# A transformer block on one core: tiles 0 and 1 as loads of their own, a new stored order, and ten waits of GpSimd on VectorE

## The chip, the cores and the metric

The kernel runs on one core of a Trainium2 chip. The metric is the time of one execution on the device, in microseconds (us), as the median of several runs. The profile is of one execution; its span is the time from the first to the last instruction on the core. Engines are named as in the profile: PE is TensorE's matmul, PEld its weight load, DVE is VectorE, ACT is ScalarE, POOL is GpSimd, SP is SyncE, which here only issues DMAs (SPq).

## What is computed

The input `x` is one batch of S = 2048 rows of D = 448 values in bf16. The block is an attention layer with 16 heads of 28 values and softmax feature maps, followed by a gated feed-forward layer with F = 1792, each behind a layer norm and with a residual:

```python
q, k, v = heads(ln(x) @ wqkv)
pq, pk = q @ w_phi, k @ w_phi                      # per head, 28 x 28
phi_q = concat(softmax(pq), softmax(-pq))          # 56 features
phi_k = concat(softmax(pk), softmax(-pk))
kv, z = phi_k.T @ v, sum_rows(phi_k)               # over all 2048 rows
o = (phi_q @ kv) / (phi_q @ z + 1e-6)
h = x + merge(o) @ wo
out = h + (sigmoid(ln(h) @ w_gate) * (ln(h) @ w_up)) @ w_down
```

`kv` and `z` sum over all rows, so no row's attention output can be formed before the keys and values of all rows are done. The feed-forward part needs no such sum.

## The kernel before

**Tiles and stages.** The 2048 rows are 16 tiles of 128 rows, taken singly or in pairs (`pr`). The stages are:

- Loads and weights. `x` tiles are loaded by `load_x` (`("x", t0)`), `wk` in two pieces, `w_phi` (`wph`), `wv`, `wq` in four and `wo` in eight (`wom`). `w_phi` is folded into the key and query weights: `kT` (PE transpose, L539), `WkT` (copy), `wM` (matmul, L554), `W2` (copy). For the query weights the transpose is a DMA (`wqT`, L500) on SP's queue, from `wq_raw` to `WqT`.
- First layer norm, tile by tile: `bst` (statistics, L582), `agg` (L584), `ve`, `rstd` (a power on POOL, L587), for later tiles `mm` and `nm` (L590, L592), then `xn` (L601 on ACT, L602 on DVE). The normed tile is transposed into `xnT`: tiles 0 to 3 by PE (`xP`, L612, and a copy `xT`), the others in pairs by a DMA on SP (`xT`, L620).
- Keys and values: `pa` and `pb` (L636) are the two halves of a tile's projection (`va`, `vb` for the values of tiles 0 and 1); a `b` half waits for its `a` half. ACT takes the two exponentials `ekp` and `ekm` (L656, L658); `v1` is a copy. DVE sums them (`ss`, L677) and inverts the sums (`rs`, L681); `phi` (L683) multiplies, on DVE or on POOL. `kv` (L695) adds the tile into one bank of PSUM, tile after tile.
- Queries: `qa` and `q` (L735) for a chunk of four tiles and half of the heads, then `eqp` and `eqm` (L745) on ACT, 1024 columns each.
- When all of `kv` is summed, `kvz` (L750, DVE) masks it. `num` (L771) is a tile's numerator and denominator; `ocp` (L424, a copy out of PSUM) is on ACT or DVE. DVE divides in six steps (`rSm`, `rr`, `b`, `c`, `rd`, `o`, L787 to L799), `od` (L818) pads, and `oT` transposes: for pair 0 on PE (`oP`) with copies, otherwise by a DMA (L820).
- Output projection `woa`, `wo_` (L832) for a pair; for pair 0 the residual is added on PE (`wr`, L840), and `hc` copies the sum. For the others DVE adds it (`h`, L862). Then the second layer norm: `bst2`, `agg2`, `ve2` (L870), `rstd2` (POOL, L872), `hn` (L876) and the transpose `hT` (pair 0: `hP` on PE, L886, and copies; others: DMA, L894).
- Feed-forward in chunks of 2, 4, 4, 4 and 2 tiles: `ga` and `gu` (L933) are the gate and up products of one of 14 slices of F, `sig` (ACT, L942) and `hh` (DVE, L950) gate them, `dn` (L967) multiplies with `w_down`, `fin` (L974) adds the residual and `st` stores a tile. The `wd` loads each wait for a `gu` of the first chunk.

**What sets the order.** Every step is a task with an engine (or a choice of two, `engs`), its dependencies and, on PE, a choice of PSUM banks. `ORDER` is a stored list of numbers, one a task: the number divided by 32 is the task's place in the order of creation, its last two bits choose the engine, and the three bits above choose the banks. `stored` reads the list, `emit` walks through it and appends each task to its engine's queue, in front of it the waits that it needs. A wait is on a semaphore that counts the finished tasks of an engine (or on that of a DMA). Each engine runs its queue strictly in order, so an instruction that waits holds up all that stands behind it. A task that takes a bank also waits for the task that emptied that bank last. On PE, dependencies between its own tasks need no wait, apart from a `b` half on its `a` half. Waits of SP hold up the DMAs behind them in the same way.

The task list of before has 884 tasks. POOL's queue has 47 of them: constants, `Wp`, `ve`, `mm`, `rstd`, `nm`, ten of the sixteen `phi`, and the `rstd2` with two `ve2`. DVE has 304, ACT 169, PE 288 and SP 76.

Of the kernel before, what the change touches and what calls it, by code (L numbers as in the profile page):

```python
# [86 lines left out]
"""  # L87


class _Task:  # L90
    __slots__ = ("name", "eng", "occ", "lat", "fn", "deps", "rank", "kind", "banks", "until", "got",
                 "start", "finish", "idx", "bias", "need", "size", "after", "rows", "pace", "behind", "engs")


class _Graph:


    ENGINES = ("sp", "act", "pe", "dve", "pool")
# [222 lines left out]
def build(nc, A_x, A_wqkv, A_w_phi, A_wo, B_w_gate, B_w_up, B_w_down, out):  # L321
# [7 lines left out]
    for n in SIZES:  # L329
        t0 = CH[-1][0] + CH[-1][1] if CH else 0  # L330
# [10 lines left out]
    with ExitStack() as es:  # L341
# [130 lines left out]
        def load_x(t0, t1, **kw):  # L472
            load(("x", t0), x_sb[:, t0:t1, :], x_t[:, t0:t1, :], size=112.0 * (t1 - t0), **kw)
            for t in range(t0, t1):
                x_ld[t] = ("x", t0)
# [552 lines left out]
```

## Time and profile before

| what | value |
|---|---|
| median of 3 runs | 206.85 us (205.95 to 206.87) |
| the profiled execution | 205.79 us |
| its span | 204.0 us |
| PE busy | 196.3 us (96%) |
| DVE busy | 135.3 us (66%) |
| ACT busy | 94.7 us (46%) |
| POOL busy | 34.5 us (17%) |
| bytes read from HBM, written | 8.98 MB, 1.84 MB |
| granted TensorE clock, mean | 1.00 |

The span has 1.79 us less than the execution's own time; the rest lies before the first and after the last instruction. In the profile, a line of a group gives the operation, what it writes and reads, how many there were, the busy time and the mean duration of one; in a timeline each row begins with the start and the duration, and ends with the idle time of the engine before it and what ended that. PE's matmuls are pipelined, so durations of neighbours overlap, and the time of one is better read from start to start.

### The profile page before, as it was taken

To read this page: it belongs to the slowest core of one execution; us is meant where nothing else is said; L and a number is where in the kernel's file an instruction comes from. 1 tells how busy PE (TensorE), PEld (TensorE's weight loads), DVE (VectorE), ACT (ScalarE), POOL (GpSimd) and SP (SyncE) were. 2 spreads that over 40 slices of the span, in tenths; PEclk is the share of its full clock that TensorE was granted. 3 is DMA by queue.
4 is the path that set the end of the run, shared out by engine and by line. 5 is a ranking of instruction groups with operands and counts; after the bars stand their busy time and mean duration, and the time that the engine had idled before them with its cause. 6 is when DMAs were issued, how large, how long until landed. Compare 5 with 4: busy or idle time off the path is not lost.

```text
span 204.0 us, 5395 instructions
## 1 busy us (share of the span) xinstructions
PE 196.3 (96%) x2276; PEld 109.2 (54%) x2276; DVE 135.3 (66%) x304; ACT 94.7 (46%) x169; POOL 34.5 (17%) x51
## 2 busy tenths in 40 slices
PE   7998998998889999999999999999999999999994
PEld 2544554555436985554445555454444555786553
DVE  2979999996999995789949846722455313541412
ACT  2699997999999462444031441202234400442000
POOL 5626973680000300003000100110000000000000
PEclk9999999999999999999999999999999999999999
DMA  5998797673040394311250020050020000200141
GB/s 153 310 289 133 170 152 128 173 245 125 3 101 5 80 190 118 99 45 31 51 127 5 0 51 3 1 125 3 0 74 3 2 0 3 69 3 0 33 158 59
DMA packets 35109, 16.94 MB, mean 83 GB/s; under 512 B 26828, under 2 KB 34060, under 8 KB 35084
## 3 DMA queue, kind: packets, MB, share of 16 engines
q1 hardware_dynamic: 34812, 16.36, 33.7%
q8 instruction: 18, 0.29, 0.6%
q10 hardware_dynamic: 272, 0.23, 0.3%
q14 instruction: 7, 0.06, 0.1%
HBM read 8.98 MB, written 1.84 MB: 53 GB/s over the span
## 4 chain that ended last, share of the span: by engine, by line
PE 81%; DVE 6%; DMA 5%; ACT 4%; SPq 3%; issue 1%; DVEq 0%
PE bank L933 42%; PE bank L967 21%; PE bank L636 5%; PE bank L832 5%; PE bank L735 4%; DMA WqT<-wq_raw 3%; SPq L460 3%; DMA wq_raw<-in_A_wqkv_dram 2%; PE bank L695 2%; DVE phi L683 1%; PE bank L771 1%; ACT v L424 1%; ACT ek L656 1%; ACT ek L658 1%; SPq L500 1%
## 5 line engine op out<-in xcount | busy, mean ns | idle before, releaser
L933 PE MATMUL bank<-xnT,wg_sb 64*128 64x512 bf16 (+1 forms) x490 | 87.5, 333 | 0.2 <-issue 0.2
L933 PE MATMUL bank<-xnT,wu_sb 64*128 64x512 bf16 (+1 forms) x490 | 87.6, 333 | 0.0
L942 ACT ACTIVATE sg_sb<-bank 128x512 f32<-128x512 f32 (+1 forms) x70 | 34.7, 511 | 81.5 <-PE bank L933 75.7
L950 DVE SCALAR_TENSOR_TENSOR hh<-sg_sb,bank 128x512 bf16<-128x512 f32 (+1 forms) x70 | 39.0, 575 | 30.4 <-ACT sg_sb L942 28.2
L933 PEld LDWEIGHTS bank<-xnT,wg_sb 64*128 64x128 bf16 x490 | 45.0, 94 | 20.9 <-issue 3.0
L933 PEld LDWEIGHTS bank<-xnT,wu_sb 64*128 64x128 bf16 x490 | 44.8, 94 | 14.0
L967 PE MATMUL bank<-wd_sb,hh 128*128 128x448 bf16 (+1 forms) x238 | 43.1, 342 | 0.0
L967 PEld LDWEIGHTS bank<-wd_sb,hh 128*128 128x128 bf16 x238 | 22.9, 98 | 20.1 <-DVE hh L950 0.4
L974 DVE SCALAR_TENSOR_TENSOR x_sb<-bank,x_sb 128x448 bf16<-128x448 f32 (+1 forms) x17 | 9.9, 594 | 24.6 <-PE bank L967 24.5
L636 PE MATMUL bank<-Wk,xnT 64*128 64x448 bf16 x112 | 21.7, 350 | 0.2
L636 PE MATMUL bank<-Wv,xnT 64*128 64x448 bf16 x112 | 21.9, 350 | 0.0
L683 POOL TENSOR_TENSOR phi<-ek,rsum 128x896 bf16<-128x896 bf16 x10 | 17.8, 1784 | 8.0 <-DVE rsum L681 7.4
L677 DVE TENSOR_REDUCE ssum<-ek 128x32 f32<-128x896 bf16 x16 | 16.5, 1064 | 0.4 <-ACT ek L656 0.4
L745 ACT ACTIVATE eq<-bank 128x1024 bf16<-128x1024 f32 x16 | 16.7, 1070 | 0.2
L872 POOL TENSOR_TENSOR rs<-rs,neghalf 128x2 f32<-128x2 f32 x8 | 5.6, 697 | 60.0 <-DVE rs L870 59.8
L735 PE MATMUL bank<-xnT,Wq 64*128 64x512 bf16 x112 | 14.3, 377 | 0.0
L832 PE MATMUL bank<-wo_sb,oT 64*128 64x448 bf16 x112 | 13.0, 350 | 0.7 <-DVE rs L870 0.6
L424 ACT CAST opm<-bank 128x960 bf16<-128x960 f32 x13 | 12.1, 976 | 1.4 <-PE bank L771 1.4
L636 PEld LDWEIGHTS bank<-Wk,xnT 64*128 64x128 bf16 x112 | 9.2, 94 | 6.1 <-PE bank L636 1.5
L636 PEld LDWEIGHTS bank<-Wv,xnT 64*128 64x128 bf16 x112 | 9.2, 94 | 4.8 <-ACT WkT L424 0.3
L862 DVE TENSOR_TENSOR x_sb<-bank,x_sb 128x896 bf16<-128x896 f32 x7 | 7.5, 1085 | 3.4 <-PE bank L832 3.4
L658 ACT ACTIVATE ek<-bank 128x448 bf16<-128x448 f32 x16 | 8.8, 558 | 1.2 <-PE bank L636 1.1
(92 smaller groups left out, 170.5 us busy)
## 6 DMA issues: line engine op xcount, KB each, us to landing
wu_sb<-in_B_w_up_dram SPq DMA_DIRECT2D x4, 448.0 KB, 3.5
wg_sb<-in_B_w_gate_dram SPq DMA_DIRECT2D x4, 448.0 KB, 4.2
out_dram<-x_sb SPq DMA_DIRECT2D x15, 112.0 KB, 1.8
wd_sb<-in_B_w_down_dram SPq DMA_DIRECT2D x7, 224.0 KB, 3.0
x_sb<-in_A_x_dram SPq DMA_DIRECT2D x2, 448.0 KB, 4.5
x_sb<-in_A_x_dram SPq DMA_DIRECT2D x3, 224.0 KB, 4.4
wq_raw<-in_A_wqkv_dram SPq DMA_DIRECT2D x4, 128.0 KB, 3.7
Wv<-in_A_wqkv_dram SPq DMA_DIRECT2D x2, 224.0 KB, 4.6
```

The lines of the kernel that those rows point to most:

```text
L424: return e.copy(dst, src) if hasattr(e, "activation") else e.tensor_copy(dst, src)
L636: r = e.matmul(bank[bk][:, 0:D], lhsT=half(xnT, hi)[:, t, k, :], rhs=half(w, hi)[:, k, :], start=(i == 0), stop=(i == 6), tile_position=(6 ...
L658: task(("ekm", t), "act", act_p(D), lambda e, t=t, s=s: e.activation(ek[:, s, 1, :], bank[got(k_at[t][0])[k_at[t][1]]][:, 0:D], ACT.Exp, s ...
L677: task(("ss", t), "dve", dve(896), lambda e, s=s: e.tensor_reduce(ssum[:, s, :].rearrange("p (a h) -> p a h", h=2), ek[:, s].rearrange("p ...
L683: task(("phi", t), None, 1.68, lambda e, t=t, s=s: e.tensor_tensor(phi[:, t % NPHI, :, :, 0:DH, :].rearrange("p a g d h -> p (a g) d h"), ...
L735: r = e.matmul(bank[bb[j]], lhsT=half(Wq2, hi)[:, k, 2 * g:2 * g + 2].rearrange("p c d h -> p (c d h)"), rhs=half(xnT, hi)[:, 4 * c:4 * c ...
L745: task((key, gp, c), "act", act_p(1024), lambda e, gp=gp, c=c, sg=sg, nm=nm: e.activation(eq[c][:, sg, 2 * gp:2 * gp + 2, :], wide[got(nm) ...
L832: r = e.matmul(bank[bb[j]][:, 0:D], lhsT=half(oT, hi)[:, pr % NO, j, k, :], rhs=half(wo_sb, hi)[:, k, :], start=(i == 0 and not res), stop ...
L933: r = e.matmul(bank[b][:, 0:N], lhsT=half(w, hi)[:, k, fs], rhs=half(hnT, hi)[:, t0:t0 + n, k, :], start=(i == 0), stop=(i == 6), tile_pos ...
L942: task(("sig", f_, c), "act", act_p(N), lambda e, j=j, N=N, nm=nm: e.activation(sg_sb[:, j % NSG, 0:N], bank[got(nm)[0]][:, 0:N], ACT.Tanh ...
L950: task(("hh", f_, c), "dve", dve(N), lambda e, j=j, N=N, nm=nm, f_=f_, c=c: e.scalar_tensor_tensor(hhT[c % 2][:, f_, 0:N], sg_sb[:, j % NS ...
L967: r = e.matmul(bank[b][:, c0:c1], lhsT=hhT[c % 2][:, f_, o:o + P], rhs=wd_sb[:, f_, c0:c1], start=(f_ == 0), stop=(f_ == FT - 1))
```

## The change

Three things are changed.

1. `load_x(0, 2)` becomes `load_x(0, 1)` and `load_x(1, 2)`: tiles 0 and 1 have a DMA each (task `("x", 1)` is new, so all later tasks move by one place). The two places that had taken tile 0's load for both tiles, `wr` and `h`, now name both loads.
2. `ORDER` is replaced by another list. All queues change. The table shows the tasks that change engine.

| engine | no longer there | newly there |
|---|---|---|
| SP | `wk`(1), `x`(6) | `x`(1) |
| ACT | `xT`(0), `W2`(1,3), `xn`(7), `xn`(8), `v1`(12), `ocp`(2), `oT`(0,0), `hT`(0,0) | `wk`(1), `x`(6), `xn`(6), `xn`(14), `v1`(13), `ocp`(0), `ocp`(3), `ocp`(8) |
| POOL | `ve`(12), `nm`(12), `phi`(4), `phi`(10), `phi`(14), `ve2`(4) | `ve`(1), `ve`(2), `ve`(4), `mm`(4), `phi`(5), `phi`(13), `ve2`(7) |

What POOL or ACT lose goes to DVE, and what they gain comes from it (the loads apart). PE keeps its 288 tasks in another order. The parts of the new queues that the prediction speaks of:

```
SP, before: x0 wk1 wk0 x4 wph x6 wv1 wv0 wom0 wq3 wq2 wq1 wq0 x8 x12 wqT1 wqT0 xT4 xT6 ...
SP, after:  x1 x0 wph wk0 x4 wq2 wv1 wq3 wv0 wq1 wq0 x8 wom1 x12 wqT1 wom4 wqT0 xT4 xT6 ...
ACT, before: x2 | ACT, after: x2 wk1 x6
SP later, before: oT1 oT2 wd1 oT3 wd3 wd0 hT1 hT2 wd5 oT4 ...
SP later, after:  oT1 oT2 hT1 wd1 oT3 wd0 hT2 wd3 wd2 wd5 wd4 oT4 ...
PE around WqT, before: pa2 pb2 wM(0,1) wM(0,3) wM(0,2) pa5 pa4 pb5 ...
PE around WqT, after:  pa2 wM(0,0) wM(0,1) wM(0,2) pb2 pa4 wM(0,3) pb4 pa5 ...
PE at kvz, before: kv15 qa(0,3) num0 num1 num2 q(0,3) num3 num4 num5 num6 qa(0,2) qa(1,2) num7 ...
PE at kvz, after:  kv15 qa(0,2) num3 num2 num1 num0 qa(0,3) num5 num7 q(0,2) num6 num4 q(0,3) ...
ACT at kvz, before: ocp1 ocp2 ocp4 ocp5 ocp6 eqp(0,3) ocp7 eqp(1,2) oT(0,0) eqp(0,2) ...
ACT at kvz, after:  ocp3 ocp1 ocp0 ocp5 ocp7 ocp6 ocp4 eqp(0,2) eqp(0,3) eqm(0,2) ...
```

3. `TURNS` lists ten pairs. When the queues are written, the first task of a pair (on POOL) also waits for the second (on DVE).

```diff
+TURNS = [(('rstd', 2), ('xn', 0)), (('rstd', 4), ('xn', 3)), (('phi', 1), ('xn', 9)), (('phi', 2), ('xn',
+         10)), (('rstd', 12), ('phi', 3)), (('phi', 5), ('phi', 4)), (('phi', 7), ('xn', 15)), (('phi', 12),
+         ('phi', 10)), (('rstd2', 2), ('od', 3)), (('rstd2', 6), ('o', 7))]
...
         done = self.stored(ORDER) if ORDER.strip() else self.order()
+        for name, first in TURNS:
+            self.tasks[name].need.append(first)
         queues = {e: [] for e in self.ENGINES}
...
-        load_x(0, 2, bias=BIG, engs=EITHER)
+        load_x(0, 1, bias=BIG, engs=EITHER)
+        load_x(1, 2, bias=BIG, engs=EITHER)
...
-                task(("wr", pr), "pe", 0.38, fr, [x_ld[t0], "ident"], banks=PAIRS,
+                task(("wr", pr), "pe", 0.38, fr, [x_ld[t0], x_ld[t0 + 1], "ident"], banks=PAIRS,
...
-                    [("wo_", pr), x_ld[t0], ("xn", t0), ("xn", t0 + 1)])
+                    [("wo_", pr), x_ld[t0], x_ld[t0 + 1], ("xn", t0), ("xn", t0 + 1)])
```

92 rows, old and new, of the table ORDER are left out of this document.

## The prediction

> **What bounds the kernel now.** I read the page first, then a table of each engine's busy time in five stretches, cut at marks of the chain of waits: the first projection after `WqT` (18.3 us), `kvz` (46.8), the first GLU matmul (65.0), the second GLU chunk (78.0).
>
> ```profile
> span 204.0 us, 5395 instructions
> ...
> PE 196.3 (96%) x2276; PEld 109.2 (54%) x2276; DVE 135.3 (66%) x304; ACT 94.7 (46%) x169; POOL 34.5 (17%) x51
> ```
>
> ```profile
> core 0: us, PE busy (x) PEld busy (x) DVE busy (x) ACT busy (x) POOL busy (x), PEclk, DMA share, GB/s
> 0.00:18.30 18.30, 16.42 (x132) 7.59 (x132) 13.31 (x44) 12.48 (x25) 8.80 (x27) 1.00 0.97 235
> 18.30:46.80 28.50, 27.90 (x487) 15.23 (x488) 27.07 (x51) 26.18 (x49) 19.32 (x14) 1.00 0.75 169
> 46.80:65.00 18.20, 16.03 (x326) 8.64 (x326) 17.34 (x41) 17.51 (x22) 0.69 (x1) 1.00 0.22 57
> 65.00:78.00 13.00, 12.83 (x257) 11.35 (x250) 12.19 (x36) 7.17 (x18) 1.65 (x3) 1.00 0.65 134
> 78.00:204.00 126.00, 123.13 (x1094) 66.41 (x1094) 65.38 (x137) 31.39 (x60) 4.06 (x6) 1.00 0.16 40
> ```
>
> In a row the stretch and its length come first, then busy time by engine. PE (TensorE) is the bound of the whole: 126 us of the 204 are GLU matmuls that no edit touches. The change removes no matmul, so it can win only PE's idle time: 18.30 - 16.42 = 1.88 us in the first stretch, then 0.60, 2.17 and 0.17; the 2.87 of the last are nearly all after the last matmul (201.14). Idle time between 18.3 and 78 is thus 2.94 us, the ceiling of what a better order can win there. From 18 to 65 us DVE and ACT are 95% busy too, so an order has little room. The waits behind the idle time, from PE's timeline (idle time and its releaser in brackets):
>
> ```profile
> 17.55 0.76 PE L554 MATMUL bank<-Wp,WqT 112*128 112x112 bf16 x12 [0.51 <-DMA WqT<-wq_raw]
> ...
> 31.41 0.44 PE L695 MATMUL bank<-v,phi 128*64 128x58 bf16 x16 [0.60 <-DVE phi L683]
> ...
> 50.11 0.40 PE L771 MATMUL bank<-kvz,eq 64*128 64x60 bf16 x16 [0.26 <-ACT opm L424]
> 51.00 0.40 PE L771 MATMUL bank<-kvz,eq 64*128 64x60 bf16 x16 [0.49 <-DVE opm L424]
> ...
> 56.17 0.54 PE L840 MATMUL bank<-x_sb,ident 128*128 128x448 bf16 x2 [0.61 <-DVE oT L424]
> ...
> 60.99 0.74 PE L832 MATMUL bank<-wo_sb,oT 64*128 64x448 bf16 x6 [0.58 <-DVE rs L870]
> ```
>
> **The stall that the turns aim at.** The view of the tile `phi` (minimum, median, maximum in ns):
>
> ```profile
> L683 POOL TENSOR_TENSOR phi<-ek,rsum x10: 1682/1692/2148, 18.5 to 43.4; 128x896 bf16<-128x896 bf16 x10
> L683 DVE TENSOR_TENSOR phi<-ek,rsum x6: 558/586/2105, 28.8 to 45.2; 128x896 bf16<-128x896 bf16 x6
> ```
>
> The two extremes meet: POOL's `phi`(7) runs from 28.72 to 30.87 and DVE's `phi`(3) and `phi`(5) from 28.77 to 31.35. `phi`(3) delays POOL by 2148 - 1682 = 0.47, and then POOL holds `phi`(5) up by 2105 - 558 = 1.55; `kv`(5) waits on PE. In the other overlaps (POOL at 39.66 and 43.43, 1.94 each) it is POOL that loses, by 0.26. So one of many meetings cost DVE anything. [...]
>
> **The terms, on PE's time, against this execution.**
>
> 1. Front, to 18.3 us. `x`(1) alone is 112 KB where 224 KB landed at 4.19, and its statistics lead: up to 0.3 us sooner on DVE. Against that, `wk`(0) (issued 1.93, landed 4.4 later, first transpose of it at 6.41) now has `w_phi` and `x`(6) before it, 249 KB at the page's 300 KB a us: 0.8 later, 7.2. ACT gets both queues' work back: `xT`(0) and `W2`(1,3) go to DVE, two copies of 0.45 from start to start, so `W2` is complete at 6.41 + 0.8 + 5.4 - 0.9 = 11.7, as now (11.81). `WqT`: `wq`(2) and (3) have some 324 KB fewer ahead of them, so the first transpose can issue about 1.0 before 10.45; but `x`(12) is still ahead of it in the rings, and `wom`(4) (0.83) now stands between the two transposes. I take the second to land at 17.2 instead of 17.50 (ends: 16.4, and 17.7). Behind it come three `wM` (0.2 each) and now also `pb`(2) (0.57), which before had run ahead of it: the next projection at 17.2 + 1.2 = 18.4, against 18.29. **+0.1 us** (-0.2 to +0.8, the upper end where `wk`(0)'s 0.8 is not made up).
>
> [...]
>
> 2. 18.3 to 46.8. Idle 0.60 now, all at `kv`(5). Here `phi`(5) goes to POOL with a turn behind `phi`(4), and (4), (10), (14) to DVE, 7 on DVE for 6: DVE gives back 1.55 and takes on 0.56 for a `phi`, 0.3 for `ve`(12) and `nm`(12). The stall goes. What is late next: `pa`(11) comes 0.57 sooner (`pb`(9) stands behind it) and needs the banks that ACT frees with `eqm`(0,0) at 29.10, where PE reaches it now at 29.26; some 0.2 us come back. The six turns here (`phi` 1, 2, 5, 7, 12 and `rstd` 12) hold up POOL's queue: behind `phi`(1) and (2) stand `rstd`(12) and `nm`(12), hence `xn`(12), (13), a transpose on SP and the last projections; but POOL is idle for 9.2 us of the 28.5. **-0.4 us** (-0.6, the whole idle time, to +0.6, the same stall made once more by a turn).
>
> 3. 46.8 to 65. Idle 2.17, every gap behind a copy, or a chain of them, on ACT or DVE. `ocp`(0), (3) and (8) go from DVE (1.15 each) to ACT (0.96, 0.88 apart back to back), `ocp`(2) the other way, and the copies `oT`(0,0) and `hT`(0,0) (0.67, 0.60) from ACT to DVE. ACT: 2 x 0.88 - 0.67 - 0.60 = +0.49; DVE: 0.42 + 0.41 - 2 x 1.15 = -1.47. ACT is the busier now (17.51 of 18.20) and gets fuller: seven `ocp`, 7 x 0.88 = 6.2 us, stand ahead of the last four `eq` pairs. The value is nearer to ACT's row: **+0.3 us** (-1.2, where DVE's relief decides, to +0.5).
>
> 4. 65 to 78. `num`(10) moves behind the first GLU matmul, as work (0.24) neither won nor lost; the 0.17 before the second chunk may go. **-0.1 us** (-0.2 to +1.0, see the second rival).
>
> 5. From 78: the same matmuls, last half tile and store; `rstd2`(6)'s turn behind `o`(7) delays tiles whose chunk starts some 5 us after their transpose lands. **0** (±0.2).
>
> Sum: +0.1 - 0.4 + 0.3 - 0.1 = **-0.1 us**, so 205.7 for the profiled execution's 205.79 (204.0 span and 1.79 around it). The median shown, 206.85, is 1.06 above it: **206.7 us**.
>
> **Rivals.** First, faster: the order's balance counts, DVE's 1.47 us in stretch 3 and the stall in 2. For it: DVE releases two of the last four gaps above. Against: ACT is as full. -0.2 - 0.6 - 1.2 - 0.2 = -2.2 at best, about -1.5 likely: 205.3. Chance 0.26.
>
> Second, slower: `hT`(2) lands after its turn. Before the second chunk SP now issues `hT`(1), `wd`(1), `oT`(3), `wd`(0), `hT`(2): each of the last two transposes has a 224 KB load just ahead. A lone transpose lands 2.7 us after issue (`oT`, page), but the one issued at 72.25 behind two such loads took 4.8. Issued at 73.9 it would land at 78.7 instead of 76.6; PE is there at 78.1. With `oT`(3) late for `woa`(3) as well that is +1.0, on top of term 1 at +0.5 and the rest as forecast: +1.4, 208.2. It decides once such a transpose takes over 4.2 us. For it: that 4.8. Against: one load ahead of each, not two. Chance 0.22.
>
> Third, the turns don't do what they say: DVE is held up elsewhere, since all meetings moved. Price 0.60 again, -0.1 becomes +0.5: inside the forecast's band.
>
> **Chances and range.** The measurement can tell about 0.5%, 1.0 us, from no change. Forecast (with the third rival): 0.52, its own range 205.8 to 207.9. Faster 0.26, slower 0.22. The range takes in most of both rivals and the unknown ends: 205.0 to 208.2.
>
> **What would show it.** Right: no `phi` on DVE above 0.7 us; PE's idle time in stretch 2 under 0.4 and in stretch 3 again 2 to 2.7; first GLU matmul at 64.7 to 65.3. Term 1: first transpose of `wk` near 7.2, `wM`(0) near 17.2. Second rival: a gap of over 0.5 before `woa`(3) or the first matmul of the second chunk, released by a DMA. It is wrong if stretch 3 loses a microsecond of idle time, or if the `WqT` transposes move by more than 0.8.

## The result, and the profile after

The changed kernel takes 209.2 us (median of 18 runs, 206.74 to 212.99), the kernel before 206.78 in the same series (18 runs, 205.95 to 209.13). The ratio is 1.0089 with a 95% interval of 1.0066 to 1.0113: 0.89% of 206.8 is 1.8 us, slower. The ratio leaves out the four runs of the changed kernel that took over 1.5% longer than its fastest (210.87 to 212.99 us); with them the medians lie 2.4 us apart. The forecast, no change at 206.7, was wrong, and the result lies above its range (to 208.2). The profiled execution of the changed kernel took 208.05 us with a span of 206.3, the one before 205.79 and 204.0. That of the kernel before lies 1 us under its median and below all its 18 runs; that of the changed kernel lies near the middle of its nine runs at an undisturbed clock (median 208.0, see e5_filled). So the two traces show where time is lost, but with 2.3 us they show some 0.5 us more of it than the ratio's 1.8.

The page of the changed kernel, and its busy time in the five stretches of the prediction (the columns are those shown there):

```profile
span 206.3 us, 5402 instructions
...
PE 195.5 (95%) x2276; PEld 106.5 (52%) x2276; DVE 135.7 (66%) x305; ACT 93.5 (45%) x167; POOL 31.7 (15%) x52
```

```profile
0.00:18.30 18.30, 13.61 (x112) 6.96 (x112) 13.96 (x42) 10.30 (x20) 8.90 (x29) 1.00 1.01 221
18.30:46.80 28.50, 28.43 (x454) 15.21 (x456) 26.62 (x53) 25.57 (x50) 16.90 (x14) 1.00 0.72 178
46.80:65.00 18.20, 15.81 (x344) 8.62 (x337) 16.45 (x40) 18.17 (x22) 0.70 (x1) 1.00 0.22 56
65.00:78.00 13.00, 12.78 (x268) 10.59 (x264) 11.40 (x34) 8.30 (x17) 1.59 (x3) 1.00 0.44 87
```

PE was busy 13.61 us of the first stretch (16.42 before) and 28.43 of 28.50 in the second (27.90 before): the loss is in the front, and the stall of the second stretch is gone. In the third, ACT is busy 18.17 of 18.20.

Stretches cut at fixed times hold different work in the two kernels. So I cut both traces at the same steps of PE's queue, and where one kernel had still to do a step that the other had done, I add that step's time:

| mark on PE | before | after | later by | still owed | loss so far | of this stretch |
|---|---|---|---|---|---|---|
| first `wM` for the query weights | 17.55 | 18.37 | 0.82 | `pb`(2), 0.57 | 1.39 | **+1.39** |
| `kv`(15) | 46.35 | 47.31 | 0.96 | | 0.96 | **-0.43** |
| first GLU matmul | 65.01 | 66.58 | 1.57 | `num`(10), 0.24 | 1.81 | **+0.85** |
| second GLU chunk | 77.98 | 80.17 | 2.19 | | 2.19 | **+0.38** |
| span | 204.0 | 206.3 | 2.3 | | 2.3 | **+0.1** |

The waits on PE that stand behind this (start, duration, and in brackets the idle time and its releaser):

```profile
18.37 0.76 PE L562 MATMUL bank<-Wp,WqT 112*128 112x112 bf16 x12 [1.52 <-DMA WqT<-wq_raw]
...
50.17 0.40 PE L779 MATMUL bank<-kvz,eq 64*128 64x60 bf16 x16 [0.45 <-ACT opm L431]
...
53.62 0.40 PE L779 MATMUL bank<-kvz,eq 64*128 64x60 bf16 x16 [0.45 <-ACT opm L431]
...
78.50 0.93 PE L840 MATMUL bank<-wo_sb,oT 64*128 64x448 bf16 x8 [0.67 <-DMA oT<-o_pad]
```

The first was 0.51 before. The next two stand behind copies on ACT; they are two of seven waits between `kv`(15) and the first GLU matmul that come to 2.31 us (five and 2.10 before). The last is `woa`(3), held by its transpose, as the second rival had it. A tail hides in the durations: a `num` takes 0.23 from start to start when the next matmul follows at once, and 0.40 when PE then waits, so by these two figures a stop costs about 0.17 that counts as busy, beside the idle time shown.

Why the query weights' transposes came late is read from SP's timeline (start, duration of the issue, what). First the changed kernel, then the kernel before:

```profile
8.34 0.59 SPq L467 DMA_DIRECT2D x_sb<-in_A_x_dram  x1
8.97 0.83 SPq L467 DMA_DIRECT2D wo_sb<-in_A_wo_dram  x1
9.86 0.40 SPq L467 DMA_DIRECT2D x_sb<-in_A_x_dram  x1
10.38 1.33 SPq L508 DMA_TRANSPOSE WqT<-wq_raw  x1
11.76 0.87 SPq L467 DMA_DIRECT2D wo_sb<-in_A_wo_dram  x1
12.73 1.69 SPq L508 DMA_TRANSPOSE WqT<-wq_raw  x1
```

```profile
8.48 1.60 SPq L460 DMA_DIRECT2D x_sb<-in_A_x_dram  x2
10.45 3.54 SPq L500 DMA_TRANSPOSE WqT<-wq_raw  x2
```

`wq`(2) and `wq`(3), which the first transpose needs, had landed at 9.89 (10.44 before), but SP reached it only at 10.38, because it was still issuing. The `wo` load in the middle, `wom`(4), puts the second transpose at 12.73 (11.88 before). It lands at 18.32 (17.50 before).

### The profile page after: what moved, and what is told of

It reads as the page before. It is cut to its first block, busy times and chain, and to the rows that moved or that the text cites. A ratio compares the mean times of both kernels' runs of the same rounds, so it can differ in the third digit from the quotient of the medians.

```text
span 206.3 us, 5402 instructions
## 1 busy us (share of the span) xinstructions
PE 195.5 (95%) x2276; PEld 106.5 (52%) x2276; DVE 135.7 (66%) x305; ACT 93.5 (45%) x167; POOL 31.7 (15%) x52
## 4 chain that ended last, share of the span: by engine, by line
PE 78%; DVE 8%; SPq 5%; DMA 5%; issue 1%; POOL 0%; ACT 0%; POOLq 0%
PE bank L941 37%; PE bank L975 21%; PE bank L644 8%; SPq L467 5%; PE bank L840 4%; PE bank L743 3%; DMA WqT<-wq_raw 3%; DMA oT<-o_pad 2%; PE bank L703 2%; DVE b_sb L802 1%; DVE b_sb L799 1%; DVE o_pad L807 1%; SPq L508 1%; DVE hh L958 1%; DVE opm L431 1%
## 5 line engine op out<-in xcount | busy, mean ns | idle before, releaser
L950 ACT ACTIVATE sg_sb<-bank 128x512 f32<-128x512 f32 (+1 forms) x70 | 34.2, 512 | 79.8 <-PE bank L941 73.5
L941 PEld LDWEIGHTS bank<-xnT,wu_sb 64*128 64x128 bf16 x490 | 45.3, 94 | 16.6
L691 POOL TENSOR_TENSOR phi<-ek,rsum 128x896 bf16<-128x896 bf16 x9 | 15.2, 1690 | 10.1 <-DVE xn_pad L610 3.4
L753 ACT ACTIVATE eq<-bank 128x1024 bf16<-128x1024 f32 x16 | 15.8, 1073 | 0.6 <-PE bank L743 0.6
L431 ACT CAST opm<-bank 128x960 bf16<-128x960 f32 x15 | 13.6, 982 | 4.4 <-PE bank L779 4.4
L590 DVE BATCH_NORM_STATS2 st<-x_sb 128x6 f32<-128x448 bf16 x16 | 9.3, 610 | 2.9 <-DMA x_sb<-in_A_x_dram 2.9
```

The source lines that it names most:

```text
L431: return e.copy(dst, src) if hasattr(e, "activation") else e.tensor_copy(dst, src)
L691: task(("phi", t), None, 1.68, lambda e, t=t, s=s: e.tensor_tensor(phi[:, t % NPHI, :, :, 0:DH, :].rearrange("p a g d h -> p (a g) d h"), ...
L753: task((key, gp, c), "act", act_p(1024), lambda e, gp=gp, c=c, sg=sg, nm=nm: e.activation(eq[c][:, sg, 2 * gp:2 * gp + 2, :], wide[got(nm) ...
L941: r = e.matmul(bank[b][:, 0:N], lhsT=half(w, hi)[:, k, fs], rhs=half(hnT, hi)[:, t0:t0 + n, k, :], start=(i == 0), stop=(i == 6), tile_pos ...
L950: task(("sig", f_, c), "act", act_p(N), lambda e, j=j, N=N, nm=nm: e.activation(sg_sb[:, j % NSG, 0:N], bank[got(nm)[0]][:, 0:N], ACT.Tanh ...
```

## The experiments

All are timed against the kernel before, by ratios with 95% intervals; 0.1% is 0.2 us. My theory: the order's places in the front, in the third stretch and at `oT`(3) cost the time, and the turns nothing. Rivals: the turns hold POOL back; or an idle PE lowers its own clock.

### The turns alone taken out (e1_no_turns)

```diff
-TURNS = [(('rstd', 2), ('xn', 0)), ...
+TURNS = []
```

> The changed kernel with an empty list of turns; the order and the split loads stay. My theory is that the 1.8 us are lost in three places of the order (the query weights' transposes and pb(2) behind them in the front, about 1.2 us; an ACT that is busy 18.17 of 18.20 us between 46.8 and 65, about 0.6; oT(3) late for woa(3), about 0.7) and that the turns cost and win next to nothing: within 0.4 us of the changed kernel, so about 1.0085 of the kernel before. The rival: the turns hold POOL's queue back (rstd, nm and so xn behind them), and the time is theirs: 1.5 us or more comes back, 1.002 or less. The opposite is possible too: without the turns two or three phi on DVE rise above 1.5 us and it becomes slower by 0.5 to 1.5 us.

Measured 1.0109 (1.0061 to 1.0157): the loss stays, so the turns are not its cause. DVE's `phi` in this run (minimum, median, maximum in ns):

```profile
L687 DVE TENSOR_TENSOR phi<-ek,rsum x7: 560/564/624, 26.7 to 46.6; 128x896 bf16<-128x896 bf16 x7
```

None is long. It was 2105 at most in the kernel before, and 626 in the changed one. So the new order removed the stall; with it, the turns had nothing left to do.

### One turn in the kernel before (e13_before_turn)

```diff
+        self.tasks[("phi", 7)].need.append(("phi", 5))
```

> The kernel before with one turn: phi(7) on POOL also waits for phi(5) on DVE, the pair that meets at 28.7 us there (phi(5) takes 2.11 us in place of 0.56, and kv(5) waits 0.60 on PE). If a turn does what it says, no phi on DVE is above 0.7 us, the 0.60 before kv(5) goes, and the kernel is 0.3 to 0.6 us faster (0.997 to 0.9985). The rival: the stall goes, but PE then waits the 0.6 at the next place (ACT and DVE are over 90% busy there), and the time stays within 0.2.

Measured 0.9981 (0.9961 to 1.0), and no stall before `kv`(5):

```profile
L682 DVE TENSOR_TENSOR phi<-ek,rsum x6: 556/586/624, 31.6 to 47.8; 128x896 bf16<-128x896 bf16 x6
```

A turn does what it says where the two engines do meet. What it is worth in time, some 0.4 us, is not clear of zero.

### pb(2) ahead of wM (e2_pb2)

```diff
 PE:
-pa2 wM(0,0) wM(0,1) wM(0,2) pb2 pa4
+pa2 pb2 wM(0,0) wM(0,1) wM(0,2) pa4
```

> The changed kernel with pb(2) ahead of the first wM for the query weights on PE, as the kernel before has it. In the changed kernel PE idles some 1.7 us before that wM (18.37 us) and then takes 0.57 for pb(2) ahead of the next projection. If that placing is part of the loss, 0.5 us comes back (1.0064 of the kernel before) and the next projection starts near 19.1 in place of 19.64. The rival: ACT and DVE, over 90% busy until 65 us, set the pace behind 18 us and not PE: 0 to 0.2 us comes back.

Measured 1.0102 (1.0071 to 1.0133): nothing came back, though not for the rival's reason. `pa`(4) then waited 1.26 us for its own input, `xT`(4), the next transpose on SP, which landed at 20.41 (19.32 in the changed kernel, where `pa`(4) did not wait for it).

### The two wo loads behind the transposes (e3_wqT, e6_front, e8_before_wom)

```diff
 SP, e3_wqT:
-... wq0 x8 wom1 x12 wqT1 wom4 wqT0 xT4 xT6 wom3 ...
+... wq0 x8 x12 wqT1 wqT0 wom1 wom4 xT4 xT6 wom3 ...
 SP, e6_front (and pb2 ahead of wM, as in e2_pb2):
+... wq0 x8 x12 wqT1 wqT0 xT4 xT6 wom1 wom4 wom3 ...
 SP, e8_before_wom, the kernel before:
-... wq0 x8 x12 wqT1 wqT0 xT4 xT6 ...
+... wq0 x8 wom1 x12 wqT1 wom4 wqT0 xT4 xT6 ...
```

> The changed kernel with the loads wom(1) and wom(4) moved behind the two transposes of the query weights on SP, so that the transposes are issued at about 9.9 and 11.4 us in place of 10.38 and 12.73. If their lateness (landed 18.32, in the kernel before 17.50) is the main part of the loss, the second lands at 17.0 to 17.5 and 0.8 to 1.2 us comes back (1.003 to 1.005 of the kernel before). The rival: what sets the landing is not the issue but what else the 16 DMA engines carry at that time; then it lands at 18 or later and under 0.3 us comes back.

> The changed kernel with wom(1) and wom(4) behind xT(6) on SP, and pb(2) ahead of the first wM on PE. In e3_wqT the two loads stood between wqT(0) and xT(4), which landed at 19.28 and held pa(4) until 19.32; in e2_pb2 pa(4) waited for xT(4) too, until 20.46. So here xT(4) should land near 18.3 and pa(4) start near 18.6. If the row of transposes on SP is what the front hangs on, this wins what e3_wqT won and 0.5 more: 0.998 to 1.001 of the kernel before. The rival: with the front mended, the later stretches (ACT full between 46.8 and 65, oT(3) late) still cost 1.2, and it stays at 1.003 to 1.005.

> The kernel before, with only two loads moved as in the changed kernel: wom(1) ahead of x(12), wom(4) between the two transposes of the query weights. If these two loads are the main cause, the second transpose is issued near 13.4 in place of 11.88, lands 0.8 to 1.4 us later, PE idles 1.3 us or more at wM (0.51 in the kernel before), and the kernel is 0.6 to 1.6 us slower (1.003 to 1.008). The rival: the kernel before has room there, and it is within 0.4 us.

e3_wqT measured 1.0026 (1.0007 to 1.0046), e6_front 1.0000 (0.9979 to 1.0021). SP's timeline of e6_front:

```profile
9.49 3.89 SPq L506 DMA_TRANSPOSE WqT<-wq_raw  x2
13.44 3.54 SPq L626 DMA_TRANSPOSE xnT<-xn_pad  x2
```

The four transposes are issued in a row. `wqT`(0) lands at 16.91 and `xT`(4) at 17.79; PE has no wait at `wM` (17.11) and `pa`(4) starts at 17.84 (19.64 in the changed kernel). The reverse, e8_before_wom, took 1.0054 (1.0019 to 1.0089): the same two loads cost the kernel before 1.1 us, with 0.91 us of idle time at `wM`. Taken out of one kernel and put into the other, they carry most of the front's loss. One profile alone would not show it: with the two loads among the transposes, `wqT`(0) landed at 18.27 to 18.75 in five profiles of the new order (the changed kernel, e1, e2, e4, e5), and with SP's front as in e6_front at 16.08 to 18.28 in four (e6, e9, e11, e16). In e6_front the first transpose is issued as soon as its data are there (9.49, data at 9.41). Why one and the same front lands up to 2.2 us apart is open. `pb`(2) seems to be worth something only once `xT`(4) is in time; no run moves it alone on the mended front.

### The gaps filled (e5_filled), and a lowered clock (e4_oT3)

```diff
 PE, e5_filled: fill(10) made 6 matmuls, fill(11) made 7 and moved
-... pa2 wM(0,0) ...
+... pa2 fill11 wM(0,0) ...
 DVE and SP, e4_oT3:
+od3 directly behind o3 on DVE
-oT1 oT2 hT1 wd1 oT3 wd0 hT2 wd3
+oT1 oT2 oT3 hT1 wd1 hT2 wd0 wd3
```

> The changed kernel with od(3) directly behind o(3) on DVE, oT(3) ahead of hT(1) on SP, and hT(2) ahead of wd(0). oT(3) should be issued near 69 us in place of 73.47, land before 74, and PE's gap of 0.67 us before woa(3) should go. If the transposes behind wd loads are part of the loss, 0.5 to 0.9 us comes back (about 1.005 of the kernel before). The rival: what is late next, hT(2) or DVE's hn(4) and hn(5), takes the gap's place before the second chunk: under 0.2 us comes back.

e4_oT3 measured 1.0088 (1.0057 to 1.012), no gain in all. Its profile shows two things at once. From the first GLU matmul to the second chunk it needed 12.74 us (13.59 in the changed kernel), and the gap at `woa`(3) was gone. But in the front PE idled 2.24 us before `wM`, and soon after the granted clock (third column from the end) was halved; four of its six runs have a mean granted clock of 0.991 or 0.992:

```profile
18.00:20.00 2.00, 1.20 (x18) 0.82 (x18) 2.00 (x3) 0.79 (x2) 2.00 (x3) 0.95 1.41 196
20.00:22.00 2.00, 1.95 (x12) 0.44 (x8) 1.19 (x4) 1.11 (x3) 0.82 (x2) 0.50 0.44 100
22.00:24.00 2.00, 2.00 (x18) 0.98 (x18) 0.00 (x0) 1.21 (x3) 0.95 (x1) 0.70 0.68 131
```

At half clock a row of 2 us with a mean of 0.95 holds 0.2 us of it, the next 2.0, the last 1.2: 3.4 us in all, some 1.7 us of PE's time (an estimate). Is that part of the loss?

> The changed kernel with its order, and on PE 13 more filler matmuls (0.22 us each, on constants, read by nobody) in the two places of the front where PE idles: five ahead of the first kT, the one filler task moved and made seven ahead of the first wM for the query weights. Theory: in the e4_oT3 profile PE idled from 16.56 to 18.80 and the granted clock was 0.50 from about 19.9 to 23.3, which cost some 1.7 us; an idle PE in the front now and then costs a stretch of half clock, in some executions and not in others, and that is part of the changed kernel's loss and of its scatter (206.74 to 212.99). Then its slow executions go: 0.5 to 1.2 us off the median (1.002 to 1.006 of the kernel before), none above 210. The rival: the clock has no part in the median, only the late landings have; then it stays at 1.0085 or is 0.1 to 0.3 us slower through fillers that run into the landing.

Measured 1.009 (1.0061 to 1.012): PE had no gap in the front, the clock was 1.00, and the ratio stayed. So the late landings are the larger part of the loss, as the rival has it. That the clock has no part in it is not shown, and the mean granted clock of each run speaks against it. Of the 18 runs of the changed kernel, nine have 0.983 to 0.992 and took 209.09 to 212.99 us; the other nine have 0.998 or more and took 206.74 to 209.34 (median 208.0). All six runs here have 0.999 or more and took 207.38 to 209.53 (median 208.37). The fillers took the lowered clock away and, by the medians, cost some 0.4 us themselves. At an undisturbed clock the changed kernel thus loses about 1.2 us (208.0 beside 206.78); by this estimate, lowered clocks make up the other 0.6 of the ratio's 1.8. e3_wqT and e6_front, which mend the cause of the gap before `wM`, have no run under 0.998 either, in 12 each.

### oT(3) in time, on the mended front (e9_front_oT3)

```diff
 e6_front, with od3, oT3 and hT2 placed as in e4_oT3
```

> The two mends together: e6_front, and the edit of e4_oT3 (od(3) directly behind o(3) on DVE, oT(3) ahead of hT(1), hT(2) ahead of wd(0)). In e4_oT3 the time from the first GLU matmul to the second chunk was 12.74 us, in the changed kernel 13.59, but a stretch of half clock in the front hid that. If oT(3)'s lateness is a loss of its own, 0.6 to 0.9 us better than e6_front: 0.996 to 0.997 of the kernel before, with no idle time at woa(3). The rival: the idle time of 0.62 at woa(3) only moves (to the second chunk or a later one): within 0.3 us of e6_front.

Measured 0.9927 (0.9901 to 0.9953), median 205.68: faster than both kernels. SP's timeline of the changed kernel, then of this one:

```profile
71.49 1.23 SPq L902 DMA_TRANSPOSE xnT<-hn_pad  x1
72.82 0.55 SPq L467 DMA_DIRECT2D wd_sb<-in_B_w_down_dram  x1
73.47 1.59 SPq L828 DMA_TRANSPOSE oT<-o_pad  x1
```

```profile
67.08 2.12 SPq L826 DMA_TRANSPOSE oT<-o_pad  x1
70.12 1.23 SPq L900 DMA_TRANSPOSE xnT<-hn_pad  x1
```

`oT`(3) is now issued before `hT`(1), lands at 70.51 in place of 78.46, and PE has no wait at `woa`(3). The place on SP was the smaller part of its lateness, some 0.8 us: `od`(3), which pads its input, ran on DVE only at 72.48 in the changed kernel, 4.3 us after `o`(3) had ended. DVE's timeline of the kernel before, then of the changed one:

```profile
68.20 0.62 DVE L799 TENSOR_TENSOR o_pad<-b_sb,rden 128x896 bf16<-128x896 bf16 x1
...
69.40 0.19 DVE L818 COPY o_pad<-o_pad 128x128 bf16<-128x128 bf16 x1
```

```profile
67.58 0.61 DVE L807 TENSOR_TENSOR o_pad<-b_sb,rden 128x896 bf16<-128x896 bf16 x1
...
72.48 0.19 DVE L826 COPY o_pad<-o_pad 128x128 bf16<-128x128 bf16 x1
```

From the first GLU matmul to the second chunk e9_front_oT3 needs 12.74 us, 0.80 less than e6_front (13.54). The ratios differ by 0.73%, 1.5 us; the trace accounts for 0.8 of it, which is the low end of what the two intervals allow. The medians differ by 0.87 us (206.55 and 205.68).

### The copies back on their engines (e11_engines)

```diff
 e9_front_oT3, and
-ACT: ocp0 ocp3 ocp8   DVE: ocp2 oT(0,0) hT(0,0)
+DVE: ocp0 ocp3 ocp8   ACT: ocp2 oT(0,0) hT(0,0)
```

> e9_front_oT3 with the engines of six copies as in the kernel before: ocp(0), ocp(3) and ocp(8) on DVE, ocp(2), oT(0,0) and hT(0,0) on ACT; their places in the order stay. The changed kernel needs 19.27 us from kv(15) to the first GLU matmul, the kernel before 18.66 with 0.24 us more work in it, and three gaps of 0.45, 0.21 and 0.45 stand behind copies of ACT there. If the moved copies are the cause, the stretch shrinks to 18.4 to 18.8 and 0.5 to 0.9 us come back on e9_front_oT3. The rival: DVE is as full, and the gaps move from ACT's copies to DVE's divisions: within 0.3 us, or slower.

Measured 1.0054 (1.0027 to 1.0081), 2.6 us slower than e9_front_oT3: my reading failed. Of the profiles' 2.6 us, 1.63 lies in this stretch (20.90 us, 19.27 in e9_front_oT3); 0.95 lies ahead of `kv`(15), where the two kernels are the same. Eight of its twelve runs also have a mean granted clock of 0.992 (none of the eight of e9_front_oT3 is under 0.998); the other four took 207.02 to 208.42 us. The two largest gaps of this run in that stretch:

```profile
56.12 0.34 PE L813 MATMUL bank<-ident,o_pad 128*128 128x128 bf16 x3 [1.03 <-DVE o_pad L805]
...
65.56 0.72 PE L892 MATMUL bank<-ident,hn_pad 128*128 128x128 bf16 x8 [1.72 <-DVE hn_pad L882]
```

ACT's gaps turned into larger ones of DVE: in this order, these six copies are better where the changed kernel has them. From `kv`(15) to the first GLU matmul, the kernel before and then the changed one:

```profile
46.35:65.01 18.66, 16.49 (x353) 9.06 (x348) 17.35 (x41) 17.97 (x22) 0.69 (x1) 1.00 0.21 56
```

```profile
47.31:66.58 19.27, 16.83 (x338) 8.86 (x331) 17.37 (x43) 19.03 (x23) 0.70 (x1) 1.00 0.18 47
```

DVE's work is the same, ACT's is 1.06 more: the +0.49 of the copies that the prediction works out, and an exponential (`eqm`(1,1), 0.90 from start to start) that the kernel before had done ahead of `kv`(15), less 0.37 of another: 1.02. ACT is busy 19.03 us of the 19.27, so it may be what sets this stretch; that is not shown, since the one run that took work off it became slower. What is firm is the loss itself: in all four profiles with the order of before this stretch takes 18.66 or 18.67 us, and in twelve of the thirteen with the new order and the changed kernel's copies 19.26 or 19.27 (19.36 in e7_x12). Which order would shorten it was not found.

### x(12) later (e7_x12, e10_x12_wk0)

```diff
 SP, e7_x12, against e6_front:
-... x8 x12 wqT1 wqT0 xT4 xT6 wom1 ...
+... x8 wqT1 wqT0 x12 xT4 xT6 wom1 ...
 SP, e10_x12_wk0, against e9_front_oT3 (and bst14, bst15 behind ss3 on DVE):
-x1 x0 wph wk0 x4 ... x8 x12 wqT1 wqT0 xT4 xT6 wom1 ...
+x1 x0 wk0 wph x4 ... x8 wqT1 wqT0 xT4 xT6 x12 wom1 ...
```

> e6_front, with the 458 KB load x(12) behind wqT(0) on SP as well. The first wqT can then be issued as soon as wq(2) and wq(3) are there, near 9.9, and the second near 11.4 with less ahead of it in the queues; wqT(0) should land 0.5 to 1.0 sooner than in e6_front. Against it, x(12) lands later than 14.5 and xT(4) has it ahead. If it is the bytes ahead in the queues that make the transposes late, 0 to 0.6 us better than e6_front; if a transpose takes its five us anyway, the same as e6_front; if x(12) then holds xT(4) up, 0.5 to 1 worse.

> e9_front_oT3 with two more loads moved in the front: wk(0) ahead of w_phi, and x(12) behind xT(6), with its statistics bst(14) and bst(15) behind ss(3) on DVE. In e7_x12 wqT(0) took 3.1 us from issue to landing with x(12) behind it and 5.6 with x(12) ahead, but xT(4) then waited for x(12) and took 6.3. If the bytes queued ahead are what makes a transpose late, wqT(0) lands near 14.3, xT(4) near 16.5, the first wM is no longer held by a DMA, and the kernel gains 0.4 to 1.0 us on e9_front_oT3. The rival: x(12), landing near 18.5, now makes DVE late with its statistics and so the last transposes of xn; then 0.3 to 1 us worse.

e7_x12 measured 1.0062 (1.0038 to 1.0086). `wqT`(0) took 3.15 us from issue to landing, but `xT`(4), with `x`(12) ahead, took 6.3, and PE waited there:

```profile
19.42 0.36 PE L642 MATMUL bank<-Wk,xnT 64*128 64x448 bf16 x1 [1.41 <-DMA xnT<-xn_pad]
```

e10_x12_wk0 measured 0.9995 (0.9973 to 1.0017), 1.4 us slower than e9_front_oT3. `wqT`(0) landed at 17.33 as before (17.34), though it was issued 0.59 later; it took 5.26 us in place of 5.85, and not 3.15, so `x`(12) ahead of it is not the main thing that held it. And `x`(12), landing at 21.32, made `xT`(8) 2.4 us later.

### An instruction packet moved (e15_early_fetch)

```diff
-            task(("fill", i), "pe", 0.22, lambda e: e.matmul(
-                bank[5], lhsT=warm[:], rhs=warm[:, None, :].to_broadcast([P, 4, P]), start=True, stop=True),
+            def f(e, i=i):
+                if i < 3:
+                    return e.matmul(bank[5], lhsT=warm[:], rhs=warm[:, None, :].to_broadcast([P, 4, P]), start=True, stop=True)
+                for _ in range(10):
+                    r = e.matmul(bank[5][0:64, 0:60], lhsT=warm[0:64, 0:64], rhs=warm[0:64, 0:60], start=True, stop=True)
+                return r
+            task(("fill", i), "pe", 0.22, f,
```

> The changed kernel; only nine of its twelve filler matmuls on PE are made ten small ones each (64 rows, 60 columns), which puts some 81 more matmuls and weight loads ahead in PE's instruction stream and no work that anyone reads. Theory: in all fourteen profiles so far one instruction packet of 16 KB goes by between 14.8 and 16.5 us, when PE has executed 98 to 114 matmuls, and the transposes in flight then stand still for some 1.3 us; the one that landed before it (e7_x12, wqT(0)) took 3.1 us, all others 5.2 to 6.6. With 81 matmuls more ahead, that packet should come at 8 to 10 us, before the transposes; wqT(0) then takes 3.1 to 4.5 us from issue to landing in place of 5.6, PE's idle time before the first wM shrinks by 1 us or more, and the kernel is 0.6 to 1.4 us faster than the changed kernel (1.002 to 1.006 of the kernel before). The rival: the packet only happens to be there and the bytes of x(8), x(12) and the wom loads are what holds the transposes; then the packet moves and wqT(0) lands at 18 or later all the same.

The packet came at 10.03 as expected, and `wqT`(0) took 4.26 us (13.53 to 17.79) in place of 5.59. But the first transpose, `wqT`(1), issued at 10.77, took 5.94 us (5.51 in the changed kernel), with no packet between 11 and 22 us. And the edit cost more than it won: the fillers ran until 8.57, the twelve matmuls behind them took 2.25 us in place of 1.48, and PE reached `wM` only at 20.06. Four matmuls of an `xP` took 0.61 to 0.64 us here until 14.2, as in the half-clock stretch of e16_best_no_turns (0.61 and 0.63), and 0.39 or 0.40 in the changed kernel; so PE seems to have been at half clock until then, though the clock column of the profile shows 1.00. At 1.0185 (1.0157 to 1.0213) its time tells nothing of the packet.

### The split alone, and the best version without it, or without turns

e12_before_split gives the kernel before the two loads in place of one; e14_best_no_split and e16_best_no_turns take the split or the turns out of e9_front_oT3.

```diff
 e12_before_split (e14_best_no_split is the reverse):
-        load_x(0, 2, bias=BIG, engs=EITHER)
+        load_x(0, 1, bias=BIG, engs=EITHER)
+        load_x(1, 2, bias=BIG, engs=EITHER)
 e16_best_no_turns:
+TURNS = []
```

> The kernel before with the load of tiles 0 and 1 split in two, tile 1 directly behind tile 0 on SP, and nothing else. The split adds one issue of 0.42 us ahead of all other loads of SP and lets tile 0's statistics begin sooner. I expect wk(0) at about 6.8 in place of 6.37, the first kT 0.4 later, and PE's wait for the query weights' transposes covering that: within 0.4 us of the kernel before (0.998 to 1.002). The rival: the whole row of loads and transposes shifts by the added issue, and so does the end: 0.4 to 0.6 us slower (1.002 to 1.003).

> e9_front_oT3 with tiles 0 and 1 in one load again, at the place of tile 1's. In e12_before_split the split alone was 0.43% slower, with the loads from x(8) on landing 1 us later although they were issued at the same time; one profile can't tell that from chance. If the split costs by itself, this is 0.4 to 0.9 us faster than e9_front_oT3 (0.989 to 0.991 of the kernel before). If it is the statistics of tile 1 an us sooner that count, it is 0.2 to 0.6 slower (0.994 to 0.996); if wk(0) and the transposes set the front alone, the same within 0.3.

> e9_front_oT3 with an empty list of turns. In e1_no_turns no phi on DVE took more than 0.63 us without them, so they should do nothing here: the same as e9_front_oT3 within 0.3 us (0.991 to 0.994). The rival: rstd2(2)'s turn behind od(3) and those of rstd(2) and rstd(4) only hold POOL back, and 0.3 to 0.6 us more is won.

e12_before_split measured 1.0043 (1.001 to 1.0075): slower, with `wqT`(0) issued 0.16 later and landed 1.12 later (18.62). e14_best_no_split measured 0.9963 (0.9936 to 0.999), e16_best_no_turns 0.9955 (0.9931 to 0.9979), both beside 0.9927 (0.9901 to 0.9953) with all. So the split alone costs the kernel before 0.2 to 1.6 us; in the better order it costs nothing that shows, and the turns win nothing that is clear of chance. Why the loads from `x`(8) on landed 1 us later in e12_before_split stays open.

## Why the prediction was wrong

**Term 1, the front: +1.39 where +0.1 was forecast.** This step failed: "`wq`(2) and (3) have some 324 KB fewer ahead of them, so the first transpose can issue about 1.0 before 10.45". I timed the issue by its data and not by its queue. The data came 0.55 sooner (9.89, before 10.44), but SP's timeline shows its issues one behind the other in the order of its queue, an issue took 0.4 to 1.45 us there, and `wom`(1), which stands ahead of `x`(12) in the new queue of SP, was not counted at all. The transpose was issued at 10.38, only 0.07 sooner; with the two loads behind it, 9.49 in e6_front. So nothing offset the 0.83 of `wom`(4), which I had counted. The second I took to land at 17.2, at the latest 17.7; it was issued 0.85 later than before, took as long (5.59 us, before 5.62), and landed at 18.32. The 0.57 of `pb`(2) was counted rightly. `wk`(0) came at 7.78 and not at 7.2, but `pa`(0) was only 0.30 later than before, so that part was made up as forecast. That the two loads are the cause is shown by e3_wqT, e6_front and e8_before_wom; e2_pb2 shows that `pb`(2) alone is not it. That `x`(6), issued by ACT, counts among the bytes ahead of `wk`(0), issued by SP, was my estimate (0.8 us, with `w_phi`); no run shows it, since none moves `x`(6) alone. Measured was a landing of `wk`(0) 5.6 us after its issue at 2.17, in the kernel before 4.4 after 1.93.

**Term 2, 18.3 to 46.8: -0.43 where -0.4 was forecast.** Right in size and place. The reason was half right: I set the turns beside the new split of `phi` as what ends the stall, and e1_no_turns shows that the order does it alone. The ten turns win nothing that can be measured (1.0109 without them in e1_no_turns beside 1.0089, 0.9955 in e16_best_no_turns beside 0.9927, in overlapping intervals). The third rival, that DVE is held up elsewhere, did not happen.

**Term 3, 46.8 to 65: +0.85 where +0.3 was forecast,** above its bound of +0.5. The direction was right. Two parts of the sum were mis-sized: ACT's +0.49 from the copies measured +1.06, since one exponential more had slipped behind `kv`(15), and DVE's relief of 1.47 did not come (17.37 us busy, before 17.35). That ACT's row makes the 0.85 stays argued: e11_engines, which undid the moves, was slower.

**Term 4, 65 to 78: +0.38 where -0.1 was forecast.** The second rival came true in part, at `oT`(3) and not at `hT`(2), for which PE did not wait (landed 79.84, second chunk at 80.17): `oT`(3) took 4.99 us, over the 4.2 from which the rival decides, and left 0.67 at `woa`(3). I had priced it at +1.0 with 0.22 as its chance, because one load stands ahead of the transpose and not two. What I missed is that `oT`(3) is issued late in itself (73.47, before 69.62): its input `od`(3) runs late on DVE (72.48, before 69.40), and on SP it then stands behind `wd`(1).

**Term 5: +0.1 where 0 was forecast,** within its bounds.

So the second rival named one of the losses, but the front was sized at 0.1 of the 1.39 us that it cost, and the range was cut for a front that loses at most 0.8. The prediction took no account of the granted clock either: nine of the changed kernel's 18 runs have a mean granted clock of 0.983 to 0.992. The other nine have a median of 208.0, just inside the range: the front was what went wrong, and the lowered clock added to it. The text had a test for this: it is wrong "if the `WqT` transposes move by more than 0.8". They moved by 0.80 (15.09 to 15.89) and 0.82 (17.50 to 18.32).

## What to carry to other kernels

Time a moved transfer by the queue that issues it, issue by issue, before you look at its bytes or its data; here two loads of 14 and 70 KB that nobody needed yet cost over 1 us, because they stood among transposes that somebody waited for. Don't read a landing from one execution: the same front landed the same transpose 2.2 us apart. Compare two traces at the same step of the bound engine's queue, with the work still owed added, and not at the same time. A wait that keeps operations of two engines apart is worth trying where the trace shows them hold each other up, as at 28.7 us in the kernel before (2.11 us for a `phi` of 0.56); the ten here, in an order in which no `phi` on DVE took more than 0.63, won nothing.

## What the runs showed of the hardware that was not expected

**Half clock after short gaps.** Three of the eighteen profiles (before, after and sixteen experiments) have, ahead of the last matmul, a stretch at a granted clock of 0.50, each of 3.4 us: e4_oT3 after an idle PE of 2.24 us, e13_before_turn after 1.64, e16_best_no_turns after 1.22. Others idled as long without it (1.93 and 1.52 in the changed kernel). One such stretch costs 1.7 of some 206 us (half of 3.4), which is a mean clock of 0.992, so a run's mean clock tells whether it had one (an estimate). In e3_wqT, e5_filled, e6_front, e9_front_oT3 and e10_x12_wk0, whose profiles have no gap of PE over 1.03 us between its first and last matmul, none of 50 runs is under 0.998; in the changed kernel nine of 18 are at 0.992 or less, in e11_engines (largest gap 1.72) eight of 12. The line is not sharp: the kernel before, with no gap over 0.61, has 8 of the 102 runs timed beside the experiments, e8_before_wom, with 0.91, has five of 12, and e15_early_fetch, with 1.52, none of six. What decides whether a gap is followed by it is not shown.

**Transposes that stand still.** In all profiles but that of e15_early_fetch, an instruction packet of 16 KB goes by between 14.8 and 16.5 us. Where `wqT`(0) was in flight all through it, it took 4.7 to 6.6 us from issue to landing; where it had landed (e7_x12) or all but landed (e16_best_no_turns), 3.15 and 4.12; and with the packet moved to 10.03 (e15_early_fetch), 4.26. In the changed kernel, the DMA queues moved nothing between 16.5 and 17.0 us. That the packet is the cause is not shown: the one run that moved it also delayed PE, and the first transpose, `wqT`(1), took 4.64 us in the kernel before, 5.51 in the changed one and 5.94 in e15_early_fetch although no packet began while it was in flight.
